# Decay attention and a softplus feed-forward layer on one core: early decay rows from on-chip memory, two chunks of the feed-forward kept in their buffers, GpSimd off the softmax scaling

## The chip, the cores and the metric

One core of a Trainium2 chip runs the whole kernel. It has a matrix engine (TensorE, PE in the profile), three engines for everything else (VectorE or DVE, ScalarE or ACT, GpSimd or POOL), and DMA queues, of which this kernel uses the one of SyncE (SP). Each engine works through its own list in order and waits at semaphores for the others. The metric is the time of one execution in microseconds on the device; the time before is the median of three.

## The reference: what is computed

Attention over 8 batches, 8 heads, 576 positions and 64 dimensions, with a decay between positions and a causal mask; its output, 4608 tokens of 512 values, goes through a feed-forward layer 512 -> 2048 -> 512 with softplus.

```python
scores = scale * np.matmul(q, k.transpose(0, 1, 3, 2))
log_f = np.log(np.clip(f, 0.0001, 1.0))
cum = np.cumsum(log_f, axis=-1)
decay = cum[:, :, :, None] - cum[:, :, None, :]
causal = np.triu(np.ones((S, S), dtype=bool), k=1)
scores = np.where(causal, -1000000000.0, scores + decay)
scores = scores - np.max(scores, axis=-1, keepdims=True)
attn = np.exp(scores)
attn = attn / (np.sum(attn, axis=-1, keepdims=True) + 1e-09)
out = np.matmul(attn, v)
x = out.transpose(0, 2, 1, 3).reshape(B * S, H * D)
h = x @ w_in
g = np.maximum(h, 0.0) + np.log1p(np.exp(-np.abs(h)))
return g @ w_out
```

The feed-forward weights arrive as 64-bit numbers and are converted on the core.

## The kernel before

**A planner writes the order.** The Python code first makes a list of operations (`plan.add`), each with the engines that may run it, a cost on each, the operations that it comes after, and the buffers that it takes and gives back. `Plan.run` (L101) then plays this list through: again and again it takes the operation that can start first by its own clock (ties go by the place in the list), puts it on the engine on which it would end first (a `bias` holds it away from one), and emits the instruction. So each engine's fixed order follows from these costs. Loads are reckoned by `on_dma` (L176) and `dma_lag` (L181): an SP load occupies the queue for its size at 360 KB per us, and lands 2.1 us and its size later. Where the planner sees a gap of over 0.5 us on PE before the first feed-forward accumulator is taken, it fills 0.7 of it with matmuls on a mask (`fill_gap`, L1315); seven larger ones stand at the very start (`warm`, L1305, `WARM` = 7).

**Attention jobs.** The first 4 jobs ("pairs", `first`, L550) do the first 256 positions of two heads of batch 0 each, the next 8 (`rest`) the remaining positions of one head, and these 12 multiply in plain fp32. Then come 56 jobs, one for each head of batches 1 to 7 (`whole`, L535), with operands split into a high and a low part of a faster format. The decay enters the scores as two more rows of the query and key operands (rows 64 and 65 of the tile `T`): one holds the running sum `cum`, the other a constant. A job has scores (L747 in plain form, L749 and L750 in split form), a row minimum on DVE (L754), an exponential with a row sum on ACT (L774), the scaling of the rows by one over the sum (L796 on ACT, L798 on DVE or POOL), transposes on PE (L831), and the product with the values (L880 or L886).

**The decay sums** (`decay`, L358): `f` is loaded, clipped (L366), its logarithm taken (L369), and summed along 576 columns in one scan for all 64 heads (L374). The result is stored to DRAM (`cum_d`, L377), and each plain job loads its rows from there: two DMAs for two pairs (L639), two for each later job (L644, L645). All weight loads (L432) come after the first of these in the planner's list (`first_rows`). The split jobs need the sums as a high and a low part: L382 and L383 make them, L387 stores them (`aug_d`), right behind the scan.

**Scaling.** `scales` (L197) offers DVE and ACT to every job, and POOL too from the second batch on, where DVE is held back by a bias of 1.0.

**The feed-forward blocks.** Tokens go in blocks of 256 (two) and 512 (eight). Block 0 is in plain fp32 (L1024, L1147). In the others the hidden layer is worked in 16 chunks of 128: up products (L1043), softplus on ACT and DVE, and a split of the result into `gh` and `gl` (L1098). Two accumulator banks hold tokens 0 to 255 of a 512 block (tiles 0 and 1); chunk by chunk their down products follow (L1128, `down_part`), two chunks behind. For tokens 256 to 511 (tiles 2 and 3) each chunk's `gh` and `gl` are stored to DRAM (`g_d`, L1102) and, after the first half is copied out (`finish`, L1205), loaded again two chunks at a time (L1179, tiles `gh_0b` to `gl_7b`) for the same two banks (`second`, L1172). `gh` and `gl` have three buffers each. The last two blocks come when attention is over, and take two of its banks instead; they have no second half. Block units are spread between the units of the attention jobs; the last six units of a second half go between the first ones of the next block.

Of the kernel before, what the change touches and what calls it, by code (L numbers as in the profile page):

```python
# [23 lines left out]
WINDOW = 700  # L24
PLAIN = 0
WARM = 7
# [149 lines left out]
def on_dma(kb, n=1, eng="SP"):  # L176

    return On(eng, max(0.6 * n, kb / 360 if eng == "SP" else 0.0))


def dma_lag(kb, n=1, eng="SP"):  # L181
    return 0.6 * (n - 1) + 2.1 + kb / n / 360 - on_dma(kb, n, eng).cost
# [30 lines left out]
def tile_decay_attention_softplus_ffn(  # L213
# [87 lines left out]
    cum_d = dpool.tile([BH, S], F32, name="cum_d")  # L301
# [54 lines left out]
    decay_ready, cum_used, first_rows = {}, [], []  # L356

    def decay():  # L358
# [12 lines left out]
        def scan(e):  # L371

            box["c"] = buf("x32", [P, NCC, S], "cum")[0:BH, 0, :]
            e.tensor_tensor_scan(box["c"], box["f"], box["f"], 0.0, ALU.add, ALU.min)  # L374

        def store_first(e):
            e.dma_start(out=cum_d, in_=box["c"])  # L377

        def split(e):
            hl = buf("raw", [P, 2, S], "chl", F32R)  # L380
            ch, cl = box["hl"] = hl[0:BH, 0, :], hl[0:BH, 1, :]
            e.tensor_copy(ch, box["c"])  # L382
            e.tensor_sub(cl, box["c"], ch.bitcast(F32))  # L383
# [192 lines left out]
    def attention(job):  # L576
# [28 lines left out]
        def load_v():  # L605
# [14 lines left out]
            st["v"] = add_dma(v, 128 if pair else 160, takes=(vtag,))  # L620
            st["V"] = [st["v"]]

        def load32():
# [8 lines left out]

            def rows(e):
                if pair:

                    t0 = T0[number // 2 % 2].rearrange("p t s -> p (t s)")[:, 0:2048]
                    t0 = t0.rearrange("p (i t s) -> p i t s", i=4, t=2)
                    for x in range(2):
                        e.dma_start(  # L639
                            out=t0[64 + x : 65 + x, :, x],  # L640
                            in_=cum_d[bh : bh + 4, 0:256].unsqueeze(0),
                        )
                else:
                    e.dma_start(out=qk32[64:65, 0, qs:qe], in_=cum_d[bh : bh + 1, qs:qe])  # L644
                    e.dma_start(out=qk32[65:66, 1, 0:ke], in_=cum_d[bh : bh + 1, 0:ke])  # L645
# [6 lines left out]
            if not pair:  # L652
                y = add_dma(rows, 4, 2, after=[start, decay_ready["sums"]] + set_)
# [6 lines left out]
            st["T"] = [x, y]  # L660
# [66 lines left out]
        def stat_tile(ti):  # L727
# [42 lines left out]
            for a, z, acc, box in todo:  # L770
# [5 lines left out]
                x = add(on_act(z - a, 0.19, True), weight, after=mins + [st["p"]] + ps_set)  # L776
# [3 lines left out]
        def finish_stats():  # L780
# [10 lines left out]
            for ti, (_, n_q, _, pi, po) in enumerate(tiles):  # L791
# [8 lines left out]
                st["norm"].append(add(scales(ends[ti], not plain), scale, after=[r]))  # L800
# [159 lines left out]
    def ffn_block(i):  # L960
# [109 lines left out]
        def gate(u):  # L1070
# [46 lines left out]
            if ahead < ntile:  # L1117
# [5 lines left out]
        def products(e, fc, tiles, gh, gl):  # L1123

            for n, tt in enumerate(tiles):
                lh, ll = (x[:, n * P : (n + 1) * P] for x in (gh, gl))
                for m, (l, r) in enumerate(((lh, woh), (lh, wol), (ll, woh))):
                    e.matmul(  # L1128
                        st["acc", tt], l, r[fc],
                        start=fc == 0 and m == 0, stop=fc == NFC - 1 and m == 2,  # L1130
# [6 lines left out]
        def down_part(u, k):  # L1137
            box, ready, kept = st["g", u]
            fc = u * nk + k
            tags = (("acc", "acc") + late_banks)[:ahead]  # L1140

            def mm(e):
                if fc == 0:
                    begin(range(ahead), tags)
# [7 lines left out]
                products(e, fc, range(ahead), *(box[x][:, k * nt :] for x in "hl"))  # L1152

            op = add(
                on_pe32(DM * ahead) if plain else on_pe(DM, 3 * ahead), mm,
# [7 lines left out]
            if k == nk - 1:  # L1163
# [8 lines left out]
        def second(fp, k):  # L1172

            fc = 2 * fp + k

# [8 lines left out]
            def mm(e):  # L1184
                if fc == 0:
                    begin(range(ahead, ntile), ("acc",) * 2)
                products(
                    e, fc, range(ahead, ntile), *(st[x, fp][:, k * TB :] for x in ("gh", "gl"))
                )

            if k == 0:
                need = [st["kept", fc], st["kept", fc + 1]]
                d = st["second", fp] = add_dma(load, 512, 2, after=need, takes=("gh", "gl"))
                for c in (fc, fc + 1):
                    kept_read[c] = [d]
            op = add(
                on_pe(DM, 3 * (ntile - ahead)), mm, after=[st["second", fp]] + st["downs"][-1:],
                takes=("acc",) * 2 if fc == 0 else (),
            )
            st["downs"].append(op)  # L1200
            if k:
# [34 lines left out]
        downs[-1].append((0.0, lambda: finish(range(ahead))))  # L1236
        tail = []
        if ahead < ntile:
            tail = [
                (down_t, lambda fp=fp, k=k: second(fp, k)) for fp in range(NFP) for k in range(2)  # L1240
            ] + [(0.0, lambda: finish(range(ahead, ntile)))]
# [170 lines left out]
```

## Time and profile before

| | |
|---|---|
| median of three runs | 1227.53 us (1227.13 to 1228.07) |
| the profiled execution | 1227.12 us |
| its span in the profile | 1225.1 us |
| busy: PE, DVE, ACT, POOL | 1199.9, 869.5, 872.9, 137.4 us |
| DMA | 168.38 MB, 137 GB/s over the span |

Busy time is the time in which at least one instruction of an engine is in work. Matmuls are pipelined: one of 128x512 is shown with some 400 ns while the next starts after about 227. A row of the order of time gives start, duration, engine, line, operation, what is written and read, and in brackets how long the engine stood idle before and what ended that.

### The profile page before, as it was taken

Reading aid. Unit: us, or ns where it says so; the run is one execution under the profiler, and the core shown is the slowest. Engines: PE = TensorE matmul, PEld = TensorE weight load, DVE = VectorE, ACT = ScalarE, POOL = GpSimd, SP = SyncE. Lnnn points to the kernel's source line nnn. Section 1 sums busy time; section 2 is a strip of 40 time slices with the busy share of each in tenths; the row PEclk is TensorE's granted clock in tenths of the full one; section 3 lists DMA queues with packets and bytes.
Section 4 is the critical chain, followed back from the end, with each engine's and each line's share of the span. In section 5 each row is a group of like instructions: output and inputs, shape, how many; then the busy total and the mean of one; then the engine's idle time right before and its main releaser. Section 6 shows DMA issues by size and latency. Waiting matters only on the chain.

```text
span 1225.1 us, 19553 instructions
## 1 busy us (share of the span) xinstructions
PE 1199.9 (98%) x6320; PEld 993.9 (81%) x6320; DVE 869.5 (71%) x2164; ACT 872.9 (71%) x2120; POOL 137.4 (11%) x128
## 2 busy tenths in 40 slices
PE   7899999999999999999999999999999999999998
PEld 5666678888887888888888888888888888888886
DVE  6998889998787678877787778677866774223322
ACT  4676688878787788778886788788867873444543
POOL 3632012010001000110010100110010000000000
PEclk9999999999999999999999999999999999999999
DMA  7874435435446543744464446453565425211210
GB/s 199 254 207 143 137 91 153 111 90 166 128 141 179 166 133 117 228 145 128 137 197 136 141 130 197 139 168 104 153 186 155 138 80 172 69 52 52 86 52 35
DMA packets 100198, 168.38 MB, mean 137 GB/s; under 512 B 10496, under 2 KB 74008, under 8 KB 100096
## 3 DMA queue, kind: packets, MB, share of 16 engines
q1 hardware_dynamic: 100096, 167.13, 46.2%
q8 instruction: 50, 0.82, 0.3%
q14 instruction: 52, 0.43, 0.1%
HBM read 127.85 MB, written 39.24 MB: 136 GB/s over the span
## 4 chain that ended last, share of the span: by engine, by line
PE 84%; DVE 6%; DMA 4%; ACT 4%; issue 1%; SPq 1%; POOL 1%; DVEq 0%; POOLq 0%; ACTq 0%
PE h L1043 29%; PE acc L1128 28%; PE b L831 7%; PE o L886 6%; PE s L750 3%; PE s L749 3%; PE h L1024 2%; PE acc L1147 2%; PE o L880 2%; DMA raw<-in_qkT 2%; PE s L747 1%; ACT p L774 1%; DVE s L754 1%; DMA xh_st<-in_w_in 1%; DVE pl L846 1%
## 5 line engine op out<-in xcount | busy, mean ns | idle before, releaser
L1043 PE MATMUL h<-xh,wih 128*128 128x512 f32 (+1 forms) x576 | 229.5, 401 | 0.7 <-DVE pl L846 0.3
L774 ACT ACTIVATE p<-s,negm 128x288 f32<-128x288 f32 (+7 forms) x384 | 183.0, 479 | 50.3 <-DVE negm L754 46.6
L1043 PE MATMUL h<-xl,wih 128*128 128x512 f32 (+1 forms) x576 | 216.7, 379 | 0.0
L1090 DVE SCALAR_TENSOR_TENSOR h<-h,e 128x512 f32<-128x512 f32 x136 | 95.2, 700 | 136.0 <-ACT e L1082 135.9
L754 DVE CUSTOM_DVE_ANT_0 s<-s,cmask 128x288 f32<-128x288 f32 (+5 forms) x320 | 137.8, 436 | 72.1 <-PE s L750 61.6
L798 POOL TENSOR_SCALAR p<-p,rsum 128x448 f32<-128x448 f32 (+4 forms) x79 | 89.4, 1139 | 784.5 <-PE s L750 192.6
L1076 ACT ACTIVATE e<-h 128x512 f32<-128x512 f32 x144 | 85.7, 595 | 126.4 <-PE h L1043 124.5
L846 DVE TENSOR_TENSOR pl<-b,ph 128x64 fp32r<-128x64 f32 (+1 forms) x224 | 126.3, 569 | 35.0 <-ACT ph L209 33.1
L1043 PE MATMUL h<-xh,wl 128*128 128x512 f32 (+1 forms) x576 | 148.7, 380 | 0.0
L1128 PE MATMUL acc<-woh_dt_float32r,gh 128*128 128x512 f32 x352 | 143.1, 406 | 0.0
L1128 PE MATMUL acc<-woh_dt_float32r,gl 128*128 128x512 f32 x352 | 138.0, 392 | 0.0
L1128 PE MATMUL acc<-wol_dt_float32r,gh 128*128 128x512 f32 x352 | 137.3, 390 | 0.0
L831 PE MATMUL b<-ident,p 128*128 128x128 f32 x784 | 126.5, 274 | 4.8 <-POOL p L798 2.6
L1043 PEld LDWEIGHTS h<-xh,wih 128*128 128x128 f32 x576 | 108.8, 189 | 17.1 <-DVE gl L1098 0.8
L1043 PEld LDWEIGHTS h<-xh,wl 128*128 128x128 f32 x576 | 104.8, 188 | 21.7
L1043 PEld LDWEIGHTS h<-xl,wih 128*128 128x128 f32 x576 | 108.8, 189 | 14.6
L1098 DVE TENSOR_TENSOR gl<-h,gh 128x512 fp32r<-128x512 f32 x136 | 93.4, 687 | 35.1 <-ACT gh L209 34.1
L209 ACT CAST ph<-b 128x512 fp32r<-128x512 f32 (+1 forms) x171 | 85.3, 501 | 41.7 <-PE b L831 40.4
L831 PEld LDWEIGHTS b<-ident,p 128*128 128x128 f32 x784 | 94.4, 140 | 22.6 <-ACT p L796 3.5
L796 ACT ACTIVATE p<-p,rsum 128x192 f32<-128x192 f32 (+6 forms) x219 | 108.6, 556 | 3.4 <-DVE rsum L787 2.8
L749 PE MATMUL s<-T 128*64 128x64 f32 x336 | 98.2, 304 | 2.0 <-ACT p L774 1.3
L886 PE MATMUL o<-ph,vhl 128*128 128x448 f32 (+4 forms) x352 | 98.6, 294 | 0.0
(159 smaller groups left out, 2402.2 us busy)
## 6 DMA issues: line engine op xcount, KB each, us to landing
wl<-wil_d SPq DMA_DIRECT2D x72, 512.0 KB
raw<-in_qkT SPq DMA_DIRECT2D x112, 288.0 KB
g_d<-gh SPq DMA_DIRECT2D x96, 128.0 KB
g_d<-gl SPq DMA_DIRECT2D x96, 128.0 KB
vr<-in_vR SPq DMA_DIRECT2D x64, 160.0 KB
out<-ob SPq DMA_DIRECT2D x36, 256.0 KB
sto<-in_w_out SPq DMA_DIRECT2D x11, 512.0 KB
sti<-in_w_in SPq DMA_DIRECT2D x9, 512.0 KB
```

Source lines behind the costliest of these rows:

```text
L749: e.matmul(o, qA[:, q0:end], kA[:, a:z], start=True, stop=False)
L754: e.tensor_tensor_reduce(out=box["o"], in0=box["o"], in1=cmask[0:n_q, right - w : right], scale=-0.125, scalar=m0 if i else 3.0e38, op0=AL ...
L774: e.activation(o, box["o"], AF.Exp, bias=m1, scale=-1.0, accum_out=acc)
L796: e.activation(a, a, AF.Copy, scale=f_)
L798: e.tensor_scalar(a, a, f_, None, ALU.mult)
L831: e.transpose(box["ps"][:, at : at + P], pt[pi][:, c : c + P], one)
L846: e.tensor_sub(box["l"], box["ps"][:, 0:w], box["h"].bitcast(F32))
L886: e.matmul(box["ps"][:, a - g0 : z - g0], st["vhl"][:, vc, :], pbox[x][:, o : o + z - a], start=i == 0 and m == 0, stop=i == len(todo) - 1 ...
L1043: e.matmul(o, l, r, start=m == 0, stop=m == 11)
L1090: e.scalar_tensor_tensor(h, h, 0.0, box["e"], ALU.max, ALU.add)
L1098: e.tensor_sub(box["l"], box["t"], box["h"].bitcast(F32))
L1128: e.matmul(st["acc", tt], l, r[fc], start=fc == 0 and m == 0, stop=fc == NFC - 1 and m == 2,)
```

## The change

- The scan is cut in two, columns 0 to 255 and the rest. The DRAM tile `cum_d` is gone; the rows of the operands are loaded from the scan's buffer in SBUF. The first pair's two row loads go by SP's queue as before, the second pair's by ACT's. They wait for the scan's first part, and weight loads are placed behind that part and no longer behind the first row load. Value loads of the eight later plain jobs are placed behind it too.
- The split of the sums into two parts and its store move from right behind the scan to the third round of the job loop, behind the first outputs of batch 0.
- The memsets of the softmax buffers are placed behind the scan's first part, in another order, and an exponential is placed behind the memset of its own buffer, not of all.
- `WARM` goes from 7 to 3. The planner's rate of loads goes from 360 to 262 KB per us; a DMA on another queue than SP's is reckoned with 1.5 us of its engine.
- POOL is offered the scaling in batch 1 alone; in later batches DVE has the small bias again.
- In blocks with a second half, chunks 14 and 15 aren't stored and loaded again. Their down products are cut by tile: 14 and 15 for tile 0, its copy out, 14 and 15 for tile 1, its copy out; then, from the same buffers, 14 and 15 for tile 2 and for tile 3 open the second half, and the reloaded chunks 0 to 13 follow. Their `gh` and `gl` buffers are given back after tile 3.

```diff
+RATE = 262
-WARM = 7
+WARM = 3
...
-    return On(eng, max(0.6 * n, kb / 360 if eng == "SP" else 0.0))
+    return On(eng, max(0.6 * n, kb / RATE) if eng == "SP" else 1.5 * n)
...
         def scan(e):
-            box["c"] = buf("x32", [P, NCC, S], "cum")[0:BH, 0, :]
-            e.tensor_tensor_scan(box["c"], box["f"], box["f"], 0.0, ALU.add, ALU.min)
-
-        def store_first(e):
-            e.dma_start(out=cum_d, in_=box["c"])
+            c = cum[0] = buf("x32", [P, NCC, S], "cum")[0:BH, 0, :]
+            x = box["f"][:, 0:256]
+            e.tensor_tensor_scan(c[:, 0:256], x, x, 0.0, ALU.add, ALU.min)
+
+        def scan_rest(e):
+            c = cum[0]
+            x = box["f"][:, 256:S]
+            e.tensor_tensor_scan(c[:, 256:S], x, x, c[:, 255:256], ALU.add, ALU.min)
...
-        c = add(On("DVE", 1.36), scan, after=[l], takes=("x32",))
+        decay_ready["first"] = add(On("DVE", 0.63), scan, after=[l], takes=("x32",))
+        c = decay_ready["sums"] = add(On("DVE", 0.78), scan_rest, after=[decay_ready["first"]])
         give("wl", [c])
-        decay_ready["sums"] = add_dma(store_first, BH * S / 256, after=[c])
-        cum_used.append(add(NO_ENGINE, mark, after=[decay_ready["sums"]]))
-        def rest():
-            s = add(On("DVE", 1.05, 0.0, True), split, after=[c], takes=("raw",))
+        def rest(after):
+            s = add(On("DVE", 1.05, 0.0, True), split, after=[c, *after], takes=("raw",))
...
+            later = first_rows if 3 < number < nplain else []
+            st["v"] = add_dma(v, 128 if pair else 160, after=later, takes=(vtag,))
...
+            def rows2(e, x):
+                t0 = T0[number // 2 % 2].rearrange("p t s -> p (t s)")[:, 0:2048]
+                t0 = t0.rearrange("p (i t s) -> p i t s", i=4, t=2)
+                e.dma_start(out=t0[64 + x : 65 + x, :, x], in_=cum[0][bh : bh + 4, 0:256])
+
             def rows(e):
...
+                e.dma_start(out=qk32[64:65, 0, qs:qe], in_=cum[0][bh : bh + 1, qs:qe])
+                e.dma_start(out=qk32[65:66, 1, 0:ke], in_=cum[0][bh : bh + 1, 0:ke])
...
-                need = [start, decay_ready["sums"]] + set_ + T0_set[number % 4 + 1, 1]
-                y = rows_of[number] = add_dma(rows, 8, 2, after=need)
-                first_rows[:] = first_rows or [y]
+                need = [start, decay_ready["first"]] + set_ + T0_set[number % 4 + 1, 1]
+                y = rows_of[number] = [
+                    add_dma(lambda e, r=r: rows2(e, r), 4, eng="ACT" if number else "SP", after=need)
+                    for r in range(2)
+                ]
+                first_rows[:] = [decay_ready["first"]]
...
-                st["norm"].append(add(scales(ends[ti], not plain), scale, after=[r]))
+                st["norm"].append(add(scales(ends[ti], b == 1), scale, after=[r]))
...
-            if ahead < ntile:
+            if ahead < ntile and u < NFC - 2:
                 d = add_dma(keep, 256, 2, after=[h_, l_] + kept_read.get(u, []))
...
         def second(fp, k, tiles=range(ahead, ntile)):
             fc = 2 * fp + k
+            first, here = fc == NFC - 2, fp == NFP - 1
...
+                if here:
+                    g = (st["g", fc][0][x][:, TB + o :] for x in "hl")
+                else:
+                    g = (st[x, fp][:, k * TB + o :] for x in ("gh", "gl"))
+                products(e, fc, tiles, *g, first, fc == NFC - 3)
...
+            if (k or here) and tiles[-1] == ntile - 1:
                 give("gh", [op])
                 give("gl", [op])
...
         if ahead < ntile:
+            downs[-2:] = [[], []]
+            for tt in range(ahead):
+                downs[-1] += [
+                    (down_t / 2, lambda u=u, tt=tt: down_part(u, 0, [tt]))
+                    for u in (NFC - 2, NFC - 1)
+                ] + [(0.0, lambda tt=tt: finish([tt]))]
+            for tt in range(ahead, ntile):
+                tail += [
+                    (down_t / 2, lambda k=k, tt=tt: second(NFP - 1, k, [tt])) for k in range(2)
+                ]
+            tail += [
+                (down_t, lambda fp=fp, k=k: second(fp, k)) for fp in range(NFP - 1) for k in range(2)
             ] + [(0.0, lambda: finish(range(ahead, ntile)))]
...
+    ps_set = {
+        (j, i): fill(ps[j][i], 0.0, PW[i], [decay_ready["first"]])
+        for i in (3, 4, 2, 0, 1) for j in range(2)
+    }
...
-        if n == 1:
-            decay_rest()
...
+        if n == 2:
+            decay_rest(wrote[0][0][2:])
```

More of the change, by code (lines that the diff above doesn't have):

```diff
@@ L1184, in mm @@
             def mm(e):
[L1185 to L1195, printed above, removed]
+                if first:
+                    begin(tiles, ("acc",) * 2)
+                o = (tiles[0] - ahead) * P
+                if here:
[3 more added lines that the diff above has]
+                products(e, fc, tiles, *g, first, fc == NFC - 3)
+            need = []
+            if not here:
+                if k == 0:
+                    need = [st["kept", fc], st["kept", fc + 1]]
+                    d = st["second", fp] = add_dma(load, 512, 2, after=need, takes=("gh", "gl"))
+                    for c in (fc, fc + 1):
+                        kept_read[c] = [d]
+                need = [st["second", fp]]
             op = add(
-                on_pe(DM, 3 * (ntile - ahead)), mm, after=[st["second", fp]] + st["downs"][-1:],
-                takes=("acc",) * 2 if fc == 0 else (),
+                on_pe(DM, 3 * len(tiles)), mm, after=need + st["downs"][-1:],
+                takes=("acc",) * len(tiles) if first else (),
             )
             st["downs"].append(op)
-            if k:
+            if (k or here) and tiles[-1] == ntile - 1:
                 give("gh", [op])
```

55 lines of the change are left out of this document (22 added, 33 removed).

## The prediction

> **What bounds the kernel now.** I read the page first: the shares of the engines, the slices and the chain that ended last.
>
> ```profile
> span 1225.1 us, 19553 instructions
> PE 1199.9 (98%) x6320; PEld 993.9 (81%) x6320; DVE 869.5 (71%) x2164; ACT 872.9 (71%) x2120; POOL 137.4 (11%) x128
> PE 84%; DVE 6%; DMA 4%; ACT 4%; issue 1%; SPq 1%; POOL 1%; DVEq 0%; POOLq 0%; ACTq 0%
> ```
>
> TensorE (PE) is the bound, and 84% of the chain is its own work. So an edit can gain only where PE waits or does work that the result doesn't need. The split by stage shows where that is; then the same view of the filler matmuls alone.
>
> ```profile
> core 0: us, PE busy (x) PEld busy (x) DVE busy (x) ACT busy (x) POOL busy (x), PEclk, DMA share, GB/s
> 0.00:15.00 15.00, 12.65 (x57) 9.37 (x58) 7.34 (x22) 2.25 (x4) 5.61 (x21) 1.00 0.55 118
> 15.00:67.00 52.00, 42.23 (x265) 33.03 (x264) 46.40 (x119) 34.03 (x88) 27.42 (x18) 0.97 0.88 262
> 67.00:130.00 63.00, 62.95 (x278) 41.16 (x277) 57.79 (x144) 46.32 (x111) 13.86 (x8) 1.00 0.59 171
> 130.00:280.00 150.00, 146.44 (x890) 119.67 (x889) 135.23 (x358) 118.62 (x309) 18.76 (x17) 1.00 0.41 113
> 280.00:1020.00 740.00, 735.93 (x3949) 625.43 (x3947) 566.86 (x1442) 584.75 (x1466) 70.17 (x62) 1.00 0.51 151
> 1020.00:1225.00 205.00, 199.67 (x891) 165.29 (x891) 55.90 (x85) 86.90 (x145) 1.56 (x2) 1.00 0.20 67
> ...
> 15.00:67.00 52.00, 23.14 (x170) 21.61 (x171) 0.97 0.88 262
> ```
>
> From 67 us on PE is full: 0.05 us lost up to 130, 3.6 up to 280, 4.1 up to 1020, 5.3 behind that. Before 67 it is not. Between 15 and 67 it is idle for 52 - 42.2 = 9.8 us and spends 23.1 of the rest on filler matmuls (last row), so 33 of 52 us are waste. There DVE (46.4 of 52) and the DMA (share 0.88) are near full: they convert the 64-bit weights beside the first attention jobs. From 0 to 15 nothing useful is on PE at all. That makes two places to look at: the start, and the few waits of PE behind 130 us.
>
> The start: one slice of 5 us, and rows in order of time, the last of them PE's first product of the feed-forward part.
>
> ```profile
> 10.00:15.00 5.00, 5.00 (x36) 4.21 (x35) 0.15 (x1) 0.00 (x0) 0.00 (x0) 1.00 0.27 52
> ...
> 4.77 1.35 DVE L374 TENSOR_TENSOR_SCAN cum<-fs 64x576 f32<-64x576 f32 x1 [0.75 <-ACT fs L369]
> 5.02 0.47 SPq L615 DMA_DIRECT2D vr<-in_vR  x1
> 5.07 6.50 PE L1309 MATMUL warm<-cmask 128*128 128x448 f32 x14
> 6.14 0.50 SPq L377 DMA_DIRECT2D cum_d<-cum  x1
> 6.15 0.56 DVE L382 CAST chl<-cum 64x576 fp32r<-64x576 f32 x1
> 6.74 0.75 DVE L383 TENSOR_TENSOR chl<-cum,chl 64x576 fp32r<-64x576 f32 x1
> 9.86 2.65 SPq L639 DMA_DIRECT2D T<-cum_d  x4
> 12.55 0.44 SPq L432 DMA_DIRECT2D sti<-in_w_in  x1
> 14.30 3.50 PE L747 MATMUL s<-T 66*128 66x128 f32 x16
> ...
> 67.29 2.76 PE L1024 MATMUL h<-x,woh_dt_float 128*128 128x256 f32 x12
> ```
>
> From 10 to 15 us DVE is busy for 0.15 us, ACT and POOL not at all, and the DMA share falls to 0.27. Everything waits for one thing: the decay sums go out to DRAM (L377 at 6.14) and the SP queue stands until that store has landed (9.86), then issues four row loads, and only at 12.55 the first weight load. The chain of waits says the same, and leads from there through a weight load into DVE's conversions:
>
> ```profile
> 6.14 3.66 DMA cum_d<-cum
> ...
> 17.03 11.45 DMA xh_st<-in_w_in
> 28.50 0.66 ACT ti L436
> ```
>
> The waits of PE behind 130 us, and three rows of the order of time that carry half of them:
>
> ```profile
> PE b L831 <- POOL p L798: 2.6, 2, 1.4
> PE b L831 <- ACT p L796: 2.0, 3, 1.5
> ...
> 1021.01 0.33 PE L831 MATMUL b<-ident,p 128*128 128x128 f32 x1 [1.21 <-POOL p L798]
> 370.62 0.30 PE L831 MATMUL b<-ident,p 128*128 128x128 f32 x1 [1.52 <-ACT p L796]
> 370.67 0.48 PE L1128 MATMUL acc<-woh_dt_float32r,gh_0b 128*128 128x512 f32 x1
> ```
>
> Both waits stand at the end of a block's first half. The last products on tiles 0 and 1 end together, both accumulators must be copied out before the second half may take their banks, and for that while PE has nothing but a transpose whose softmax rows aren't scaled yet; right behind it the second half (gh_0b) begins. The third, 1.4 by the longest of the first row, is of the same kind. Together 1.5 + 1.4 + 1.2 = 4.1 us of the 3.6 + 4.1 that PE loses there up to 1020 and this 1.2.
>
> **The change part by part.**
>
> *Early rows.* The scan is cut after 256 columns: 1.35 x 256 / 576 = 0.60, so the first part ends at 5.37. The rows go from the scan's own buffer, with no store to wait for. SP is free at 5.02 + 0.47 = 5.49; the first pair's two row loads cost 2.65 / 4 = 0.66 each, so the second is issued at 6.15 and the first weight load at 6.8 in place of 12.55: **5.7 us earlier**. The other two row loads go to ACT's queue, about 1.3 us of issuing where ACT stands idle (2.25 of the first 15 us busy). The first scores started 14.30 - 11.95 = 2.35 us after the last row load was issued (four at 0.66 from 9.86, the last at about 11.95); by that they start at 8.5 in place of 14.30, 5.8 earlier. DVE, ACT, queue and scores all move by the same amount, so I take -5.7. Cover for it: until 67 us PE isn't the bound, so a shift of all that bounds it there is a shift of the end. Bounds: -8 (the second pair of query loads, now at 14.28, moves past the rows' and the split's issues too) and 0 (if DVE's conversions alone set 67 us).
>
> *The split of the sums, moved.* L382 and L383 leave an idle stretch for one in which DVE is 89% busy: 0.56 + 0.75 = +1.3; 0 if they fall into the rest. Their two stores leave the head of the queue; SP then often waits for DVE, so their issue costs nothing, and the rows that they feed are first wanted behind 120 us.
>
> *Warm-up.* Three matmuls in place of seven: 6.50 / 14 x 6 = 2.8 us from 5.07, done at 7.9, before 8.5. Kept seven, they would now stand in the way until 11.6. Cost 0, as the shorter warm-up ends under the wait for the rows. Whether PE is at speed by then is a rival below.
>
> *The order's clock.* The planner now reckons loads at 262 GB/s instead of 360, near the 262 that the trace shows from 15 to 67; it will place attention ahead of conversions that come late. No row shows the new order. The nearest is what DVE idles between 15 and 67: 52 - 46.4 = 5.6 us. So between -5.6 and, the same amount the other way, +5.6. I take -1, near nothing, since DVE is already 89% busy and a better order can only fill what is left.
>
> *GpSimd's scaling.* 62 of its instructions lie between 280 and 1020 us and go to DVE or ACT.
>
> ```profile
> L798 POOL TENSOR_SCALAR p<-p,rsum x79: 435/1284/1719, 161.0 to 1020.9; 128x448 f32<-128x448 f32 x25, 64x64 f32<-64x64 f32 x24, 128x320 f32<-128x320 f32 x20, 128x576 f32<-128x576 f32 x9
> L798 DVE TENSOR_SCALAR p<-p,rsum x22: 280/475/711, 17.9 to 1020.2; 128x448 f32<-128x448 f32 x6, 128x576 f32<-128x576 f32 x6, 128x128 f32<-128x128 f32 x5, 64x320 f32<-64x320 f32 x3
> L796 ACT ACTIVATE p<-p,rsum x219: 333/549/777, 18.6 to 1021.7; 128x192 f32<-128x192 f32 x32, 128x576 f32<-128x576 f32 x28, 128x448 f32<-128x448 f32 x18, 128x320 f32<-128x320 f32 x12
> ```
>
> On DVE 62 x 0.475 = 29 us; DVE idles 740 - 567 = 173 us there, so that is hidden, and each scale is ready some 0.8 us sooner. Without that slack the 29 us would be on the path. The planner also stops holding DVE back for scaling, so part of ACT's 219 moves over; that only swaps loads of 77% and 79%. The two waits on POOL are at block ends and are counted there. Price 0, between -2.0 (the waits on ACT's scaling) and +2.0 (as much again).
>
> *Chunks kept in their buffers.* The same products run, now tile by tile: tile 0's accumulator is done six matmuls before tile 1's. Twelve products of a block take 2.72 us (36 in 8.17), so six take 1.36, more than the copy (0.69):
>
> ```profile
> 1212.52 8.17 PE acc L1128 x36
> ...
> 1220.72 0.69 DVE ob L209
> ```
>
> So when tile 1 ends, tile 2's bank is free and its operands lie in SBUF: PE has 2.72 us of products in hand where it waited 1.2 to 1.5. That would cover all 4.1; I take -3, as the planner must place them there; bounds -4.1 and 0. What is late next: the reloads. Two of the three buffer pairs stay held, so the second reload is issued only when the first kept chunk is through, 0.68 + 2.72 = 3.4 us of products ahead of its use. The one that waited shows how long such a load can take:
>
> ```profile
> 370.56 0.49 SPq L1179 DMA_DIRECT2D gl_1b<-g_d  x1
> ...
> 376.14 0.50 PE L1128 MATMUL acc<-woh_dt_float32r,gl_1b 128*128 128x512 f32 x1 [0.36 <-DMA gl_1b<-g_d]
> ```
>
> 5.6 us, so 2.2 too late if nothing else is on PE. In five of the six blocks attention's matmuls lie between; I take +0.5, for the last, with bounds 0 and 6 x 2.2 = 13. The 24 stores and 12 loads that fall away were on no wait but this one.
>
> **Sum**: -5.7 + 1.3 - 1 + 0 - 3 + 0.5 = -7.9. The profiled execution took 1227.12 us (its span 1225.1 and 2.0 around it), so 1219.2; the median of the runs shown, 1227.53, lies 0.4 above it: **1219.6**.
>
> **The rivals.**
>
> *Only the start gains* (block ends lose as much elsewhere: the scaled rows are still late and PE waits one transpose further on). For it: such waits moved freely between engines in the list above. -5.7 + 1.3 - 1 = -5.4: 1222.1.
>
> *The better clock orders the start well*, and all of DVE's idle time goes: -7.9 - 4.6 = -12.5: 1215.0. For it: PE's first feed-forward product, at 67.29, needs four converted pieces of the first weight, and DVE has been at work on pieces ever since the loads came. Against: the other pieces have to be done soon after anyway.
>
> *The start is hidden*: conversions on DVE set 67 us whenever they begin. For it DVE's 89%; against it the chain quoted above, which goes through the store and a load up to 28.5. What is left is 1.3 - 3 + 0.5 = -1.2: 1226.3.
>
> *Held buffers, the slower side.* Every second half waits for its second reload. Place: the first products on gl_1b in blocks 2 to 7. Price up to 2.2 a block, 13 in all: -8.4 + 13 = +4.6: 1232.1. It decides from 1.4 a block on. For it: one of six waited even with three pairs free. Against: five halves lie among attention's matmuls.
>
> *PE is cold at the first scores.* In the trace the first warm-up loads come 0.71 apart, then 0.37:
>
> ```profile
> 6.56 0.34 PEld L1309 LDWEIGHTS warm<-cmask 128*128 128x128 f32 x1 [0.41 <-issue]
> 7.27 0.19 PEld L1309 LDWEIGHTS warm<-cmask 128*128 128x128 f32 x1 [0.37 <-issue]
> 7.64 0.19 PEld L1309 LDWEIGHTS warm<-cmask 128*128 128x128 f32 x1 [0.19 <-issue]
> ```
>
> It reaches full speed near 7.3, before the short warm-up ends. If it slipped back, the 16 first score matmuls (3.50 us) would take twice as long: -7.9 + 3.5 = -4.4, 1223.1. The Trainium skill ("TensorE: Matmul & The Clock Gate", Part 1) says that PE runs at half rate until it has been busy for about 3.4 us and falls back after an idle window of that length, with a phase that varies. By that rule a cut warm-up is a risk; the trace agrees on the factor of two and on a few microseconds of warming.
>
> **How the numbers follow.** The forecast 0.48, only the start 0.16, the well-ordered start 0.13, cold PE 0.03: these are faster, 0.80. The hidden start 0.08: within 0.2% (2.5 us, about what a measurement of this kernel tells from no change). Held buffers 0.12: slower. The range goes from 1213, a little below the well-ordered start, to 1227, past the hidden one, and leaves out the slower side.
>
> **What would show it.** Right: the first scores near 8.5 us and the first weight load near 7; PE's first feed-forward product (now 67.3) near 62; filler and idle time before it smaller by about 6; no wait over 1 us on a transpose at the block ends; no wait of over 1.4 us on gl_1b; POOL's scaling gone behind 280 us and DVE near 600 busy from there to 1020. Wrong: a first feed-forward product that still starts near 67, or waits on reloads in all six blocks.

## The result, and the profile after

The changed kernel took 1211.85 us in the median of four runs (1210.93 to 1215.35), the kernel before 1227.33 beside it: the ratio is 0.9879 with a 95% interval from 0.9858 to 0.9900. Forecast were 1219.6 and a range from 1213 to 1227. The direction was right; the gain, 15.5 us, is twice the forecast one and the time lies below the range. The profiled execution took 1211.32 us.

The page of the kernel after: span, busy time of the engines, and the chain that ended last.

```profile
span 1209.5 us, 19176 instructions
PE 1192.2 (99%) x6270; PEld 988.0 (82%) x6270; DVE 879.6 (73%) x2246; ACT 865.1 (72%) x2115; POOL 41.2 (3%) x52
PE 80%; DVE 9%; ACT 6%; DMA 3%; issue 1%; SPq 0%; DVEq 0%; ACTq 0%
```

The split by stage after, in the stretches used before; the last two rows are the filler matmuls alone and the warm-up alone, up to 130 us.

```profile
core 0: us, PE busy (x) PEld busy (x) DVE busy (x) ACT busy (x) POOL busy (x), PEclk, DMA share, GB/s
0.00:15.00 15.00, 11.93 (x58) 9.19 (x58) 8.81 (x36) 5.55 (x18) 7.85 (x25) 1.00 0.73 170
15.00:67.00 52.00, 49.48 (x273) 36.44 (x274) 49.30 (x132) 39.84 (x103) 17.96 (x13) 0.97 0.85 254
67.00:130.00 63.00, 61.31 (x265) 39.40 (x264) 55.51 (x135) 45.98 (x106) 3.32 (x3) 1.00 0.57 160
130.00:280.00 150.00, 145.76 (x904) 122.36 (x904) 138.84 (x371) 125.74 (x328) 12.12 (x12) 1.00 0.47 133
280.00:1020.00 740.00, 737.86 (x3956) 627.10 (x3955) 576.34 (x1505) 566.23 (x1430) 0.00 (x0) 1.00 0.49 142
...
0.00:130.00 130.00, 24.25 (x168) 22.13 (x168) 0.99 0.70 199
0.00:130.00 130.00, 3.23 (x6) 1.52 (x6) 0.99 0.70 199
```

The same for the kernel before, up to 130 us: all work of the engines, fillers, warm-up.

```profile
0.00:130.00 130.00, 117.83 (x595) 83.56 (x596) 111.54 (x282) 82.59 (x202) 46.90 (x47) 0.99 0.70 201
...
0.00:130.00 130.00, 29.59 (x210) 27.56 (x210) 0.99 0.70 201
0.00:130.00 130.00, 6.50 (x14) 3.12 (x14) 0.99 0.70 201
```

I call **waste** PE's idle time up to 130 us plus fillers plus warm-up. Before it was 130 - 117.8 + 29.6 + 6.5 = 48.3 us; after, 3.1 + 2.5 + 1.7 idle and 24.3 + 3.2 are 34.8. So 13.5 us less are lost at the start, where the forecast had 5.4, and that is most of the gain. PE's idle time from 130 to 1020 us falls from 7.6 to 6.4, and at the end by another 1.7. The three come to 16.4 us against 15.6 in the two spans; PE's other work takes 0.8 longer.

Where in the start? Rows in order of time after: the row loads (ACTq and SPq), the first weight load, the first scores, PE's first feed-forward product. Below them, the last step of each conversion (the sign bits, on DVE) up to that product.

```profile
5.48 1.18 ACTq L641 DMA_DIRECT2D T<-cum  x1
5.54 1.51 SPq L641 DMA_DIRECT2D T<-cum  x2
7.54 0.35 SPq L435 DMA_DIRECT2D sti<-in_w_in  x1
8.13 2.84 PE L1350 MATMUL fill<-cmask 128*128 128x128 f32 x24
10.81 3.50 PE L753 MATMUL s<-T 66*128 66x128 f32 x16
49.59 1.89 PE L1030 MATMUL h<-x,woh_dt_float 128*128 128x256 f32 x8
...
L454 DVE SCALAR_TENSOR_TENSOR woh_dt_float<-ti,woh_dt_float x8: 664/682/686, 16.4 to 49.0; 128x512 uint32<-128x512 uint32 x8
L454 DVE SCALAR_TENSOR_TENSOR wol_dt_float<-to,wol_dt_float x4: 661/674/881, 30.8 to 37.5; 128x512 uint32<-128x512 uint32 x4
```

And the same conversions in the kernel before, up to its first feed-forward product at 67.29:

```profile
L451 DVE SCALAR_TENSOR_TENSOR woh_dt_float<-ti,woh_dt_float x10: 660/680/1095, 21.1 to 65.9; 128x512 uint32<-128x512 uint32 x10
L451 DVE SCALAR_TENSOR_TENSOR wol_dt_float<-to,wol_dt_float x8: 678/686/1097, 35.4 to 62.4; 128x512 uint32<-128x512 uint32 x8
```

The first scores move from 14.30 to 10.81, by 3.5 us. The first feed-forward product moves from 67.3 to 49.6, by 17.7. Between them DVE no longer does 18 conversions but 12. So the four pairs are through earlier mostly because less stands ahead of them; how much of it is their earlier start, the experiments tell.

### The profile page after: what moved, and what is told of

Its sections match the earlier page's. It is cut to its first block, busy times and chain, and to the rows that moved or that the text cites. A ratio compares the mean times of both kernels' runs of the same rounds, so it can differ in the third digit from the quotient of the medians.

```text
span 1209.5 us, 19176 instructions
## 1 busy us (share of the span) xinstructions
PE 1192.2 (99%) x6270; PEld 988.0 (82%) x6270; DVE 879.6 (73%) x2246; ACT 865.1 (72%) x2115; POOL 41.2 (3%) x52
## 4 chain that ended last, share of the span: by engine, by line
PE 80%; DVE 9%; ACT 6%; DMA 3%; issue 1%; SPq 0%; DVEq 0%; ACTq 0%
PE h L1049 28%; PE acc L1134 26%; PE b L837 7%; PE o L892 6%; PE s L755 3%; PE s L756 3%; PE h L1030 2%; DMA raw<-in_qkT 2%; ACT p L780 2%; PE acc L1153 2%; PE o L886 2%; DVE s L760 1%; PE s L753 1%; DVE pl L852 1%; ACT p L802 1%
## 5 line engine op out<-in xcount | busy, mean ns | idle before, releaser
L1134 PE MATMUL acc<-woh_dt_float32r,gh 128*128 128x512 f32 x376 | 153.4, 408 | 0.0
L1134 PE MATMUL acc<-woh_dt_float32r,gl 128*128 128x512 f32 x376 | 147.4, 392 | 0.0
L1134 PE MATMUL acc<-wol_dt_float32r,gh 128*128 128x512 f32 x376 | 146.8, 390 | 0.0
L211 ACT CAST ph<-b 128x64 fp32r<-128x64 f32 (+1 forms) x196 | 95.8, 493 | 47.1 <-PE b L837 45.7
L1049 PEld LDWEIGHTS h<-xh,wih 128*128 128x128 f32 x576 | 108.8, 189 | 15.5 <-DVE gl L1104 0.7
L756 PE MATMUL s<-T 68*64 68x64 f32 x336 | 97.9, 296 | 0.0
L211 ACT CAST gh<-h 128x512 fp32r<-128x512 f32 x112 | 65.8, 587 | 43.2 <-DVE h L1096 38.2
```

Source lines behind the costliest of these rows:

```text
L211: (e.tensor_copy if hasattr(e, "tensor_copy") else e.copy)(out, in_)
L756: e.matmul(o, qB[0:ST, q0:end], kB[0:ST, a:z], start=False, stop=True)
L1049: e.matmul(o, l, r, start=m == 0, stop=m == 11)
L1134: e.matmul(st["acc", tt], l, r[fc], start=first and m == 0, stop=last and m == 2,)
```

## Experiments

Times are medians; a ratio is to the kernel before, run beside it, with its 95% interval. "Before" and "changed" name the two kernels. In the expectations, theory A is the prediction's (the earlier rows shift the start) and theory B its rival (the planner's rate changes the order).

### The planner's rate alone, and the early rows alone

The first edit on the kernel before:

```diff
+RATE = 262
-    return On(eng, max(0.6 * n, kb / 360 if eng == "SP" else 0.0))
+    return On(eng, max(0.6 * n, kb / RATE) if eng == "SP" else 1.5 * n)
-    return 0.6 * (n - 1) + 2.1 + kb / n / 360 - on_dma(kb, n, eng).cost
+    each = 0.6 if eng == "SP" else 1.5
+    return each * (n - 1) + 2.1 + kb / n / RATE - on_dma(kb, n, eng).cost
```

> The kernel before with one edit: the planner reckons loads at 262 KB per us instead of 360. Theory A (the prediction's: the earlier rows shift the whole start and the clock is worth about 1 us): 1226, first feed-forward product near 66 us. Theory B (the clock puts attention ahead of weight conversions, and that is the larger part of the start's gain): 1218 to 1220, first feed-forward product between 50 and 57 us with about 12 conversions before it instead of 18.

Measured: 1219.21 us, 0.9947 (0.9931 to 0.9964). PE's first feed-forward product, and the conversions up to it:

```profile
51.71 3.62 PE L1026 MATMUL h<-x,woh_dt_float 128*128 128x256 f32 x16
...
L453 DVE SCALAR_TENSOR_TENSOR woh_dt_float<-ti,woh_dt_float x6: 661/684/689, 20.6 to 47.2; 128x512 uint32<-128x512 uint32 x6
L453 DVE SCALAR_TENSOR_TENSOR wol_dt_float<-to,wol_dt_float x4: 677/679/680, 36.4 to 41.1; 128x512 uint32<-128x512 uint32 x4
```

Ten conversions and 51.7 us, though the first scores come only at 13.55, hardly earlier than before (14.30). It is one number in the planner, with which the kernel gains 7.6 us by the medians, as theory B had it.

The second edit is all of the change that concerns the decay rows, the split of the sums and the order of the memsets, with 360 KB per us and seven warm-up matmuls kept:

```diff
-            e.tensor_tensor_scan(box["c"], box["f"], box["f"], 0.0, ALU.add, ALU.min)
+            e.tensor_tensor_scan(c[:, 0:256], x, x, 0.0, ALU.add, ALU.min)
...
-                            in_=cum_d[bh : bh + 4, 0:256].unsqueeze(0),
+                e.dma_start(out=t0[64 + x : 65 + x, :, x], in_=cum[0][bh : bh + 4, 0:256])
```

> The kernel before with the early decay rows alone (scan in two parts, rows from SBUF, weight loads behind the first part, split moved to the third round, memsets reordered). Theory A: 1222, first scores at 10.8 and first feed-forward product near 62. Theory B: 1223 to 1224, scores at 10.8, but still 16 to 18 conversions before the first feed-forward product.

Measured: 1225.51 us, 0.9993 (0.9982 to 1.0004): no difference that can be measured, and less gain than either theory had forecast. First scores, first feed-forward product, conversions:

```profile
11.62 2.70 PE L753 MATMUL s<-T 66*128 66x128 f32 x12
68.14 2.86 PE L1030 MATMUL h<-x,woh_dt_float 128*128 128x256 f32 x12
...
L454 DVE SCALAR_TENSOR_TENSOR woh_dt_float<-ti,woh_dt_float x10: 673/680/1093, 16.4 to 64.5; 128x512 uint32<-128x512 uint32 x10
L454 DVE SCALAR_TENSOR_TENSOR wol_dt_float<-to,wol_dt_float x8: 660/684/884, 27.8 to 59.1; 128x512 uint32<-128x512 uint32 x8
```

The scores start 2.7 us earlier and the conversions 4.7, and yet the product comes no earlier: still 18 conversions ahead of it. One place where the time goes stands in the same profile, a row of DVE and a row of PE:

```profile
43.07 1.70 DVE L454 SCALAR_TENSOR_TENSOR woh_dt_float<-ti,woh_dt_float 128x512 uint32<-128x512 uint32 x2
...
45.58 1.54 PE L886 MATMUL o<-p,vr 128*64 128x256 f32 x4 [6.23 <-ACT p L780]
```

PE's longest wait up to the product is 6.2 us, for an exponential. That waits for a row minimum on DVE, which starts at 44.7, right behind a run of conversion steps, though PE had the last of its scores done by 32.2. In the kernel before, PE's longest wait for an exponential up to its product is 2.7. The granted clock is down to 0.50 as well, from 44 to 54 us, in the kernel before for a third of that time; what share of the loss is the clock's, no run separates.

### Each of the two taken out of the changed kernel

```diff
-RATE = 262
+RATE = 360
```

> The changed kernel with the planner's 360 KB per us back. Theory A: 1213, hardly slower than the changed kernel. Theory B: 1218 to 1220, first feed-forward product back at 60 or later.

Measured: 1225.58 us, 0.9992 (0.9983 to 1.0002), first feed-forward product at 67.84. Without the rate nearly the whole gain of the change is gone, more than either theory had forecast.

The other run takes the early rows out of the changed kernel; its decay part is that of the kernel before:

```diff
-            e.tensor_tensor_scan(c[:, 0:256], x, x, 0.0, ALU.add, ALU.min)
+            e.tensor_tensor_scan(box["c"], box["f"], box["f"], 0.0, ALU.add, ALU.min)
...
-                e.dma_start(out=t0[64 + x : 65 + x, :, x], in_=cum[0][bh : bh + 4, 0:256])
+                            in_=cum_d[bh : bh + 4, 0:256].unsqueeze(0),
```

> The changed kernel without the early decay rows (the store to DRAM, one scan, the split behind it, as before). Theory A: 1217 to 1218. Theory B: 1215 to 1216, first scores near 14.3 and first feed-forward product near 54.

Measured: 1217.67 us, 0.9931 (0.9904 to 0.9958), scores at 14.10, product at 53.06. The time is theory A's, the product comes where theory B had it. With the rate in place the early rows are worth 1217.7 - 1211.9 = 5.8 us by the medians, but this size is rough: the four runs lie in two pairs, at 1214.6 and 1214.9 (granted clock 0.999 and 0.997) and at 1220.5 twice (0.996 and 0.995), so it may be 3 or 9. By the profiles the first product comes 3.5 us earlier with the early rows, at 12 conversions in both; so of the 17.7 us by which it moves, 14.2 don't need them. Without the rate the early rows are worth nothing that can be measured. The two parts aren't a sum.

### The order by hand

If it is the order that gains, the gain must be had without the rate. The kernel before, at 360, with fewer weight pieces in the list while the four pairs are planned:

```diff
-            for _ in range(W_EACH):
+            for _ in range(W_EACH if n >= nfirst else 2):
                 if weights_left:
```

> The kernel before, planner still at 360 KB per us; one edit by hand: in the first four rounds of the job loop two weight pieces are listed per round instead of three, so that fewer conversions stand ahead of the four pairs. If the gain of the new rate is the order (attention ahead of conversions): 1218 to 1222, fewer than 14 conversions before the first feed-forward product and that product before 60 us. If the new rate gains in some other way (when loads are issued, where fillers go): 1226 to 1228, product near 67.

Measured: 1216.53 us, 0.9922 (0.9905 to 0.9938); first feed-forward product at 53.20 with 12 conversions begun. That is a gain of 10 us from the order of the list alone, more than forecast.

The same edit in the changed kernel with the rate put back to 360:

> The changed kernel with the planner at 360 KB per us, and two weight pieces listed per round instead of three in the first four rounds. If early rows only need attention ahead of conversions to gain, by whatever means: 1208 to 1212, first scores near 11 and first feed-forward product near 49. If they need the rate itself: 1215 to 1217.

Measured: 1220.92 us, 0.9952 (0.9936 to 0.9968): a miss, on the side of neither number. Its rows show that the list edit does less here:

```profile
59.30 2.86 PE L1030 MATMUL h<-x,woh_dt_float 128*128 128x256 f32 x12
...
L454 DVE SCALAR_TENSOR_TENSOR woh_dt_float<-ti,woh_dt_float x8: 672/679/1093, 15.9 to 49.9; 128x512 uint32<-128x512 uint32 x8
L454 DVE SCALAR_TENSOR_TENSOR wol_dt_float<-to,wol_dt_float x6: 680/683/1097, 29.4 to 54.9; 128x512 uint32<-128x512 uint32 x6
```

Fourteen conversions, not twelve. The changed kernel plans its weight loads from the scan's first part on; that pieces reckoned earlier are also taken earlier, ahead of the pairs, would explain this, and why the early rows alone gain nothing; but no run shows the planner's own times.

### Which use of the rate

The rate stands in two places: how long a load holds the planner's queue (1.95 us for a 512 KB piece instead of 1.42), and when it is reckoned to land (0.53 us later). One run for each, on the kernel before.

```diff
 # both
+RATE = 262
 # b_cost262
-    return On(eng, max(0.6 * n, kb / 360 if eng == "SP" else 0.0))
+    return On(eng, max(0.6 * n, kb / RATE) if eng == "SP" else 1.5 * n)
 # b_lag262
-    return 0.6 * (n - 1) + 2.1 + kb / n / 360 - on_dma(kb, n, eng).cost
+    return each * (n - 1) + 2.1 + kb / n / RATE - on_dma(kb, n, eng).cost
```

> The kernel before; 262 KB per us only in how long a load holds the planner's queue (a 512 KB piece every 1.95 us instead of 1.42), its landing reckoned as at 360. If the spacing of the pieces is what puts attention ahead: 1217 to 1220, 10 to 12 conversions before the first feed-forward product. If not: 1225 to 1227, 18 conversions.

> The kernel before; 262 KB per us only in when a load lands (0.53 us later for a 512 KB piece), the queue held as at 360. If the spacing is what counts: 1225 to 1227, 16 to 18 conversions before the first feed-forward product. If the landing is: 1217 to 1220, 10 to 12.

Measured: 1216.61 us, 0.9918 (0.9900 to 0.9937), with the holding time; 1223.90, 0.9984 (0.9972 to 0.9997), with the landing. First products of the two:

```profile
50.12 2.86 PE L1026 MATMUL h<-x,woh_dt_float 128*128 128x256 f32 x12
...
62.45 2.76 PE L1026 MATMUL h<-x,woh_dt_float 128*128 128x256 f32 x12
```

The spacing of the pieces is what lets attention in between; the later landing gives 2.5 us, where nothing was forecast. The two don't add up: both together, the first experiment, gained 7.6. (The first row is of the run with the holding time.)

The runs that take the start apart, by PE's first feed-forward product, conversions begun by then, and waste up to 130 us worked out as above:

| kernel | median us | first product | conversions | waste |
|---|---|---|---|---|
| before | 1227.3 | 67.3 | 18 | 48.3 |
| before, early rows | 1225.5 | 68.1 | 18 | 47.5 |
| changed, rate 360 | 1225.6 | 67.8 | 18 | 47.3 |
| before, later landing | 1223.9 | 62.5 | 17 | 45.1 |
| changed, 360, order by hand | 1220.9 | 59.3 | 14 | 38.9 |
| before, rate 262 | 1219.2 | 51.7 | 10 | 39.0 |
| changed without early rows | 1217.7 | 53.1 | 12 | 41.1 |
| before, longer hold | 1216.6 | 50.1 | 11 | 37.6 |
| before, order by hand | 1216.5 | 53.2 | 12 | 35.0 |
| changed | 1211.9 | 49.6 | 12 | 34.8 |

Waste up to 130 us isn't the whole time. The kernel before with the order by hand has as little of it as the changed kernel and is 4.7 us slower; from 130 to 1020 us PE idles 9.4 us in it against 6.4.

### The kept chunks

On the kernel before, the feed-forward part of the change alone:

> The kernel before with the kept chunks alone. The prediction's step: 1224 to 1225, the waits of 1.5, 1.4 and 1.2 us on transposes at block ends gone. Rival (nothing, or reloads late): 1226 to 1229.

Measured: 1223.24 us, 0.9972 (0.9962 to 0.9981). Waits of PE behind 130 us in this run, and its stretch from 280 to 1020 us:

```profile
PE s L751 <- ACT p L776: 1.3, 2, 1.1
PE b L833 <- DVE pl L848: 0.6, 1, 0.6
PE b L833 <- ACT p L776: 0.4, 2, 0.3
...
PE b L833 <- ACT p L798: 0.2, 1, 0.2
PE acc L1130 <- ACT ob L211: 0.2, 1, 0.2
...
280.00:1020.00 740.00, 738.53 (x3954) 626.50 (x3954) 567.94 (x1439) 588.26 (x1476) 70.57 (x62) 1.00 0.47 142
```

Transposes that waited 2.6 us for POOL's scaling and 2.0 for ACT's now wait 0.2 for ACT's and not at all, as far as listed, for POOL's, though POOL still scales in this kernel (70.6 us busy in the last row); one wait on the copy of an accumulator (ob) has come, 0.2. Idle time from 280 to 1020 us goes from 4.1 to 1.5, and behind 1020 from 5.4 to 3.6.

The changed kernel with all 16 chunks stored and loaded again:

```diff
-            if ahead < ntile and u < NFC - 2:
+            if ahead < ntile:
...
-            downs[-2:] = [[], []]
+        downs[-1].append((0.0, lambda: finish(range(ahead))))
```

> The changed kernel without the kept chunks (all 16 chunks stored and loaded again, both tiles finished together). The prediction's step (block ends wait 4.1 us less, 0.5 lost to reloads): 1214 to 1216, with two or more waits of over 1 us at block ends. Rival (the block ends were chance of the order): 1211 to 1213, with no such waits.

Measured: 1212.41 us, 0.9887 (0.9872 to 0.9902). By the time it can't be told from the changed kernel, and that is the rival's number. By the profile it has the waits that were forecast for it, over 1 us: two at 876 and 877 us and one at 1009, right before a second half begins (gh_0b). In the list the columns are total, count and longest:

```profile
PE b L837 <- ACT p L780: 1.9, 3, 1.1
PE b L837 <- DVE x L921: 1.4, 1, 1.4
PE b L837 <- DVE p L804: 1.2, 1, 1.2
...
280.00:1020.00 740.00, 735.47 (x3941) 626.29 (x3939) 574.00 (x1499) 566.52 (x1432) 0.00 (x0) 1.00 0.51 150
```

From 280 to 1020 us PE is busy for 735.5 us (last row), against 737.9 in the changed kernel. That is some 2 us by one profile of each, and 0.6 by the medians of four runs that scatter over 3 us. So the waits at block ends are shown in this kernel too; what they cost it stays open.

### GpSimd's scaling, and the warm-up

```diff
-                st["norm"].append(add(scales(ends[ti], b == 1), scale, after=[r]))
+                st["norm"].append(add(scales(ends[ti], not plain), scale, after=[r]))
```

> The changed kernel with GpSimd offered the scaling in every later batch again. The prediction's step (price 0, 2 either way): 1210 to 1214. Rival (GpSimd's slow scaling is what made transposes wait at block ends): 1214 to 1216, with transposes waiting on GpSimd.

Measured: 1209.00 us, 0.9860 (0.9844 to 0.9876): faster than either number, but its interval meets that of the changed kernel. So both were measured once more, side by side on one chip.

> The changed kernel once more, beside the next one on the same chip, to tell 1211.9 from 1209.0: 1211 to 1213.

> The changed kernel with GpSimd offered the scaling in every later batch. If taking GpSimd off costs time: 1208 to 1210, below the changed kernel's interval. If the 2.9 us between the two earlier medians were scatter: the same as the changed kernel, 1211 to 1213.

Measured: 1211.80 (1210.27 to 1212.01) for the changed kernel, 0.9873 (0.9856 to 0.9891); 1208.15 (1207.61 to 1208.78) with GpSimd scaling, 0.9846 (0.9830 to 0.9863). The runs don't overlap: taking GpSimd off **costs** 3.6 us here, and the forecast of no more than 2 either way was wrong. From 280 to 1020 us in these two, first the changed kernel:

```profile
280.00:1020.00 740.00, 737.10 (x3953) 626.50 (x3951) 575.64 (x1504) 565.60 (x1430) 0.00 (x0) 1.00 0.48 142
```

and with GpSimd:

```profile
280.00:1020.00 740.00, 738.65 (x3955) 627.24 (x3954) 556.26 (x1406) 581.24 (x1458) 68.26 (x61) 1.00 0.48 141
```

DVE has 19 us more to do without GpSimd and ACT 16 less. PE's waits behind 130 us in the changed kernel (this run):

```profile
PE s L755 <- ACT p L780: 2.6, 6, 0.8
PE o L892 <- DVE x L921: 0.9, 2, 0.6
PE b L837 <- DVE p L804: 0.4, 1, 0.4
```

With GpSimd the first of these is 1.2, and the second and third aren't among the listed waits. From 130 to 1020 us PE idles 4.2 + 2.9 = 7.1 us without and 3.2 + 1.4 = 4.6 with GpSimd; that is 2.5 of the 3.6. Waste up to 130 us is 35.0 and 34.2, another 0.8, and the granted clock falls to 0.50 for some 3.4 us from 16 us on in the first profile and not in the second. So not all of the 3.6 need be the scaling: among runs with a granted clock of 1.000, three of the changed kernel took 1210.27 to 1211.59 and six with GpSimd 1207.61 to 1208.78.

The changed kernel with seven warm-up matmuls:

```diff
-WARM = 3
+WARM = 7
```

> The changed kernel with seven warm-up matmuls. The prediction's step (they would end at 11.6, behind the rows): first scores near 12 instead of 10.3 to 10.8, and 1212 to 1213. Rival (PE cold with three): the same or up to 3 us faster.

Measured: 1213.89 us (1212.64 to 1216.10), 0.9901 (0.9879 to 0.9922), first scores at 12.29. The scores come where the prediction's working put them; the time is 0.9 above what was forecast and leans to slower, with intervals that overlap.

### The two ways to the order together

The changed kernel, its rate of 262 kept, with two edits from above:

```diff
-            for _ in range(W_EACH):
+            for _ in range(W_EACH if n >= nfirst else 2):
...
-                st["norm"].append(add(scales(ends[ti], b == 1), scale, after=[r]))
+                st["norm"].append(add(scales(ends[ti], not plain), scale, after=[r]))
```

> The changed kernel with 262 KB per us, two pieces per round in the first four rounds, and GpSimd offered the scaling again. If the two ways to put attention first add up: 1204 to 1207. If 262 already holds the conversions back as far as it pays: 1208 to 1211.

Measured: 1210.76 us, 0.9869 (0.9850 to 0.9888): not better than the changed kernel with GpSimd scaling alone (1208.15), so the two ways don't add up. The start is better still, the first product at 45.51 and waste 30.2 us against 34.2, but PE idles 5.8 us from 130 to 280 where that one idles 3.2, the granted clock falls to 0.50 for 3.4 us near 244 us, and the whole is 2.6 us slower. Where the rest goes stays open.

The fastest kernel of all is the changed one with GpSimd scaling in all later batches, 1208.15 us.

## Why the prediction was right or wrong

**The order's clock**: wrong, and it is the step that failed. I took -1 and bounded it by what DVE idles from 15 to 67 us, 5.6 us either way. The rate alone measured -7.6, and taken out of the changed kernel +13.7. The bound was of the wrong thing. A better order doesn't need DVE's idle time: DVE is near full from 15 to 67 us in both kernels (46.4 of 52 us before, 49.3 after), but does other work first. What the order can win is bounded by PE's waste in the stretch, 33 us in the prediction's own first view, and I had that number and didn't use it. The rival "the better clock orders the start well" had the right sign and the right evidence (four pieces are needed, more were converted), and too low a price for the same reason.

**Early rows**: -5.7 forecast. With the rate in place 5.8 measured; without it, 1.3 by the medians and nothing by the interval. The size was right only in company, and there partly by luck, as 5.8 lies in the middle of runs that say 3 or 9. The argument "DVE, ACT, queue and scores all move by the same amount, so the end moves" was false for the kernel as it stood: there the time won was lost again before the first product, in part in a wait behind DVE's conversions, as the rival "the start is hidden" said. The parts of it that were read off rows held less well than they looked: the first weight load came at 7.54, not 6.8, the scores at 10.81 (10.34 in the second profile), not 8.5. Up to 10.8 PE had the planner's fillers to do, and started the scores without a wait. The row load that the chain of waits shows, the second pair's on ACT's queue, took 3.3 us to land. The query load behind it (second row) took 6.7, and PE waited 1.3 us for it:

```profile
5.48 3.31 DMA T<-cum
8.80 6.72 DMA T<-in_qkT
```

**The split, moved**: +1.3 forecast; in the changed kernel it takes 0.45 + 0.75 us in the full stretch, 1.2 in all, but no run separates what it costs.

**Chunks kept**: -3 + 0.5 forecast, -3.3 measured on the kernel before. Place and kind were right: the waits on transposes went although the scaling engine stayed. In the changed kernel the forecast of 1214 to 1216 without it was missed (1212.4), so the size isn't confirmed there. The held buffers cost nothing visible: no wait on a reload is listed in the changed kernel's profile behind 130 us, so that rival didn't come.

**GpSimd**: 0 with 2 either way forecast, +3.6 measured. The error was to price it as load on an engine with 173 us to spare. Of the 29 us reckoned for DVE 19 came (it is busy for 576 us from 280 to 1020, not near 600), and the waits that PE has more of are on exponentials and on the sums of outputs. That DVE's spare time isn't spread as the work is would explain this, but it is an argument; no run shows it.

**Warm-up**: 0 forecast for three; seven put the scores at 12.3, as worked out (11.6 and the fillers), and the time leans to 2 us. PE was at speed at the first scores: 16 of them took 3.50 us in both kernels. But the rival "PE is cold" had something in it, a few microseconds later. The five microseconds from 15 us on, in the changed kernel and with seven warm-up matmuls (granted clock third from the right):

```profile
15.00:20.00 5.00, 4.34 (x22) 3.35 (x22) 3.35 (x12) 3.18 (x9) 0.97 (x2) 0.69 1.04 262
...
15.00:20.00 5.00, 4.54 (x28) 3.24 (x28) 4.93 (x18) 4.83 (x17) 1.59 (x2) 1.00 1.04 298
```

In both profiles of the changed kernel the clock is at 0.50 for some 3.4 us there, and six filler matmuls take 1.30 and 1.49 us instead of 0.83. Whether the short warm-up brings this on isn't shown: with GpSimd scaling (second profile) or with all chunks stored the clock stays at 1.00 there with three matmuls too, and no gain in time was measured with seven. The Trainium skill ("TensorE: Matmul & The Clock Gate", Part 1) says that PE falls back to half rate after an idle window of about 3.4 us. The trace agrees on the half rate, but in the 3.4 us before these two falls PE had stood idle for only 1.3 and 1.5 us.

**The sum**: the start measured 13.5 us of waste instead of 5.4, block ends about as forecast, GpSimd on the other side. The range missed because its low end, 1213, lay just below the well-ordered start, whose price rested on the bound for the order.

## What to carry to other kernels

Where a scheduler's costs set the order, a cost is an edit like any other: bound its worth by the waste of the engine that is late, not by the idle time of the engine whose work is reordered. Starting a chain earlier gains only if what is queued ahead of the engine that closes it doesn't grow to fill the time; look at what that engine does first, and at whether that is needed first. Two parts can each be worth little alone and much together, so a change of several parts is taken apart from both ends, one part added and one part removed.

## What was not expected of the hardware

A load of 4 KB from four partitions of one SBUF buffer into one partition of another took 3.3 us from its issue on ACT's queue to its landing, hardly less than the 3.7 us of the 144 KB store to DRAM that it replaced; what is saved is one of the two hops. The granted clock of TensorE fell to 0.50 in 16 of the 17 profiles, for some 3.4 us or two or three times as long: from 17 us in the changed kernel, from 34 in the kernel before, and from 44 to 54 with the early rows alone. Runs of one kernel differ in it: the changed kernel took 1210.93 us at a granted clock of 1.000 over the run and 1215.35 at 0.996. And a slow engine was worth keeping: from 280 to 1020 us a 128x448 scaling takes 1.42 us on GpSimd and 0.44 on DVE, and the kernel is some 3 us faster with 66 more of them on GpSimd (76 instead of 10). All shapes together, with GpSimd:

```profile
L804 POOL TENSOR_SCALAR p<-p,rsum x76: 435/1170/1779, 146.0 to 1003.5; 128x448 f32<-128x448 f32 x25, 64x64 f32<-64x64 f32 x22, 128x320 f32<-128x320 f32 x21, 128x576 f32<-128x576 f32 x6
L804 DVE TENSOR_SCALAR p<-p,rsum x18: 341/446/693, 14.8 to 1003.7; 128x448 f32<-128x448 f32 x7, 128x256 f32<-128x256 f32 x3, 64x320 f32<-64x320 f32 x3, 128x576 f32<-128x576 f32 x3
```
